# Attention on one core: the products with v of each half in two visits instead of one

## The chip, the cores and the metric

The kernel runs on one core of a Trainium2 chip. The metric is the device time of one execution in microseconds (us), the median of several runs. The program is one launch; the host only lays out the inputs.

## What is computed

The reference is an attention followed by two feed-forward parts. The change lies in the attention alone:

```python
scores = scale * np.matmul(q, k.transpose(0, 1, 3, 2))
thresh = np.max(scores, axis=-1, keepdims=True) - tau
scores = np.where(scores >= thresh, scores, -1000000000.0)
scores = scores - np.max(scores, axis=-1, keepdims=True)
attn = np.exp(scores)
attn = attn / (np.sum(attn, axis=-1, keepdims=True) + 1e-09)
return np.matmul(attn, v).astype(np.float32)
```

with 4 batches, 8 heads, 576 tokens and 64 columns per head, all float32. Its result goes as 2304 rows of 512 into a dense layer (512 to 2048 to 512, with a Mish between) and that into a soft mixture of eight small networks.

## The kernel before

The heads are worked in pairs: 16 pairs (NPR) of two heads, head 0 and head 1. A pair has 9 steps, one per chunk of 128 query rows: chunks 0 to 3 of either head, alternating, and a ninth chunk that holds the last 64 rows of both heads. The loop at L551 runs over 144 steps and 9 more that drain the pipeline; `j` is the step within a pair, `n` the pair.

The order of the work on every engine is the order in which the code issues it (`manual_schedule`), so the loop's body is the schedule. In step `i`:

- **Score group** (`emit_S`, L307), PE: negated scores of the chunk against all 576 keys, 4 matmuls of 288 columns (10 in the ninth chunk), into one of three two-bank tiles `s` (pool `ps_s`). The tile is used again three steps later, so a score group waits until the weighing of three steps before has read it.
- **Turn** (`emit_T`, L360), PE: four transposes of the weights of chunk `i - 3` (T_LAG), for keys 0 to 511, into a bank `tp` (pool `ps_t`, two banks); ACT copies it to `pT` (L94, a helper's line).
- **Reduce** (`emit_E`, L317) on DVE, the row's extreme `nm`, and after it the exp on ACT (L318).
- **Weighing** (`emit_P`, L340), DVE, of the chunk before: threshold times exp into `pab` (three buffers, each for two chunks) or, for the ninth chunk, `pr`. Then `th` (L324), a small step of DVE.
- **Tail turns** (`emit_R`, L375 and L377), PE: the last 64 keys of up to four chunks, turned together, three times a pair (part 0 in step 6, parts 1 and 2 in steps 2 and 3 of the next pair, R_AT). They go to the unused columns of the step's own `s` tile, ahead of its score group, and ACT copies them to `pTr` at the end of the step (`evac_R`).
- **Products with v** (`emit_V`, L399), PE: for half 0 (256 rows per head) and half 1 (320 rows) of a pair, five groups of keys by two heads, ten matmuls with 64 weight columns, summed in one `tp` bank, which ACT then copies to `xT`. The profile shows two records for each matmul. `pv_at` is called at three places in every step (z = 0 before the tail turns, z = 1 after the score group, z = 2 at the end); PV_0 and PV_1 name the place. Half 0 stands at the end of step 0 of the next pair, half 1 at the end of its step 4.

Around this, POOL prepares the next pair's k and q, DVE and ACT convert the first three blocks of the dense layer's weights in some steps (CONV, CVN: L161, L164, L169), and after the last pair of a batch the sums' reciprocals are turned on PE (`norm_b`, L419; NORM_AT), go through DRAM and come back as factors. After the 16 pairs the dense layer follows (L483 to L485, L647 to L649), in the drain its first matmuls stand between the last turns and products.

Of the kernel before, what the change touches and what calls it, by code (L numbers as in the profile page):

```python
# [8 lines left out]
F32 = mybir.dt.float32  # L9
# [15 lines left out]
NPR = B * NP  # L25
# [7 lines left out]


T_LAG = 3
PV_0 = 29
PV_1 = 14
R_AT = (6, 2, 3)
NORM_AT = (0, 4)
CONV = (4, 6, 13, 15, 22, 24, 31)  # L40
CVN = (9, 45, 81)
DRAIN = (1, 2, 7, 8, 3)
# [22 lines left out]
def pow2(n):  # L65

    return 1 << (n.bit_length() - 1)
# [3 lines left out]
def kernel(  # L71
# [21 lines left out]
    def copy_act(dst, src):  # L93
        act.activation(out=dst, in_=src, func=ACTF.Copy)  # L94
# [7 lines left out]
    tp = ctx.enter_context(tc.tile_pool(name="tp", bufs=2))  # L102
# [5 lines left out]
    ps_t = ph2.enter_context(tc.tile_pool(name="ps_t", bufs=2, space=PSUM))  # L108
# [75 lines left out]
    def spans(t0, n):  # L184
        a = t0
        while a < t0 + n:
            blk = a // BT
            e = min(t0 + n, (blk + 1) * BT)
            yield blk, a - blk * BT, a - t0, e - a
            a = e  # L190
# [194 lines left out]
            copy_act(tr[:64, 256:320], ps[:64, 0, :64])  # L385
            copy_act(tr[64:, 256:320], ps[64:, 1, 64:])

    def emit_V(n, half):

        b, hp = divmod(n, NP)  # L390
        w = 256 if half == 0 else 320
        t, tr = pT[n, half]
        vt, vrt = V[n]
        pv = ps_t.tile([128, 512], F32, name="tp")
        for kc in range(5):
            for h in range(2):
                hs = slice(64 * h, 64 * h + 64)
                lhsT, rhs = (vt[:, kc, h], t[:, kc, h]) if kc < 4 else (vrt[:, h], tr)
                pe.matmul(pv[hs, :w], lhsT=lhsT, rhs=rhs, start=(kc == 0), stop=(kc == 4))  # L399
        for blk, x0, p0, ln in spans(b * S + 256 * half, w):  # L400
            copy_act(xT[blk][:, hp, x0:x0 + ln], pv[:, p0:p0 + ln])

    def pv_at(i, z):

        n, k = divmod(3 * i + z, 27)
        for nn, half, place in ((n, 0, PV_0), (n - 1, 0, PV_0), (n - 1, 1, PV_1)):
            if place == k + 27 * (n - nn) - 27 * half and 0 <= nn < NPR:
                emit_V(nn, half)

    def norm_a(b):  # L410
        r = p1.tile([128, 36], F32, name="rr", bufs=2)
        dve.tensor_scalar(out=r, in0=rs[b], scalar1=1e-9, scalar2=None, op0=ALU.add)
        dve.reciprocal(out=r, in_=r)
        rinv[b] = r

    def norm_b(b, i):
        o = SH if i < NCH else 0
        ps = st[i]["s"][:36, 0, o:o + 128]
        pe.transpose(ps, rinv[b], ident)  # L419
        return lambda: norm_out(b, ps)  # L420
# [80 lines left out]
    with tc.manual_schedule():  # L501
# [49 lines left out]
        for i in range(NCH + 9):  # L551
            n, j = divmod(i, 9)
            live = i < NCH
            if live or j in R_AT[1:]:
                st[i] = {"s": ps_s.tile([128, 2, 512], F32, name="s")}
            R = None
            pv_at(i, 0)
            if n < NPR and j == R_AT[0]:
                R = (n, 0, i)
            if n >= 1 and j in R_AT[1:]:  # L560
                R = (n - 1, R_AT.index(j), i)
            if R:
                emit_R(*R)
            turn_out = None
            if n >= 1 and (n - 1) % NP == NP - 1:
                if j == (NORM_AT[1] if n < NPR else R_AT[2]):
                    turn_out = norm_b((n - 1) // NP, i)
            if live:
                emit_S(i)
            pv_at(i, 1)  # L570
            if T_LAG <= i < NCH + T_LAG:
                emit_T(i - T_LAG)
# [4 lines left out]
            if live:  # L577
# [11 lines left out]
                for m in range(NWA):  # L589
# [3 lines left out]
                    if z in CONV:  # L593
                        cv[m][CONV.index(z)]()
                        if z == CONV[-1] and m + 1 < NWA:
                            early_w(m + 1)
            pv_at(i, 2)
            if n >= 1:
                m = n - 1
                b, hp = divmod(m, NP)  # L600
                if hp == NP - 1 and j == (NORM_AT[0] if n < NPR else 0):
                    norm_a(b)
# [273 lines left out]
        for c0, w in COLS:  # L876
            n = pow2(1024 // w)
# [104 lines left out]
        for g in range(NF, NG, 2):  # L982
            blk, m = divmod(g, NF)
            prev = [g - 1] if g == NF else [g - 2, g - 1]
            plan = TRIPLES_0 if g == NF else TRIPLES_1 if m == 2 else TRIPLES
# [387 lines left out]
```

## Time and profile before

| | |
|---|---|
| median of 3 runs | 755.63 us (754.92 to 756.26) |
| the profiled execution | 755.94 us, its span 754.2 us |
| granted clock of TensorE, mean | 0.99 |
| PE busy | 728.1 us (97%) |
| DVE, ACT, POOL busy | 519.9, 459.1, 391.9 us |

PE is the matmul row, PEld its weight loads, which partly overlap the matmuls. A matmul's end is modelled, so the distance from start to start is the better measure of what PE takes. In rows of the timeline, the text in brackets is the idle time before the row and what ended it; a row with x4 stands for four instructions that follow each other. The first 300 us are the attention, the rest the two feed-forward parts.

### The profile page before, as it was taken

The numbers are of one execution on the slowest core, as the hardware profiler recorded it, in microseconds if no ns is written. First come the engines' busy times: TensorE is split into PE (matmuls) and PEld (weight loads), VectorE is DVE, ScalarE is ACT, GpSimd is POOL, SyncE is SP. The second block draws the span as 40 slices with busy tenths as digits, with TensorE's granted clock in tenths as the row PEclk, the third lists the DMA queues.
The fourth block names the chain that finished last, engine by engine and source line by source line (L and its number), as shares of the span: only waits on it lengthen the run. The fifth ranks groups of instructions, "written<-read, shape, count | busy, mean of one in ns | idle before, by whom it ended". The sixth has DMA issues, their size and how long they took to land.

```text
span 754.2 us, 12760 instructions
## 1 busy us (share of the span) xinstructions
PE 728.1 (97%) x4641; PEld 596.0 (79%) x4641; DVE 519.9 (69%) x1018; ACT 459.1 (61%) x880; POOL 391.9 (52%) x395
## 2 busy tenths in 40 slices
PE   8999999999999999999999999999999999999995
PEld 6777777777777778998999888887898888898443
DVE  7888888888888883656986756568867545754413
ACT  6877787777777775444464655566646555644213
POOL 6665567666647733333645755465755454544000
PEclk8999999999999999999999999999999999999998
DMA  7422443433313203343330100000006111259798
GB/s 246 134 81 83 154 127 98 124 126 107 128 56 97 81 4 126 113 143 137 112 112 1 63 1 1 1 1 0 1 1 232 69 57 56 94 218 370 251 397 296
DMA packets 45678, 84.85 MB, mean 113 GB/s; under 512 B 6048, under 2 KB 21040, under 8 KB 45616
## 3 DMA queue, kind: packets, MB, share of 16 engines
q1 hardware_dynamic: 45344, 83.88, 32.8%
q8 instruction: 36, 0.59, 0.3%
q14 instruction: 26, 0.21, 0.1%
q10 hardware_dynamic: 272, 0.16, 0.1%
HBM read 79.23 MB, written 4.79 MB: 111 GB/s over the span
## 4 chain that ended last, share of the span: by engine, by line
PE 75%; DVE 13%; issue 6%; ACT 5%; DMA 1%; SPq 0%; POOL 0%; ACTq 0%
PE tp L399 11%; PE s L647 8%; PE s L649 8%; PE s L648 8%; DVE pab L340 7%; PE s L307 7%; PE tp L742 5%; PE tp L744 4%; PE tp L743 4%; PE tp L483 3%; PE tp L485 3%; PE tp L484 3%; PE tp L360 2%; PE hp L1195 2%; DVE nm L317 2%
## 5 line engine op out<-in xcount | busy, mean ns | idle before, releaser
L307 PE MATMUL s<-kb,Q 128*128 128x288 f32 (+2 forms) x672 | 126.0, 316 | 10.2 <-DVE pab L340 4.6
L317 DVE TENSOR_REDUCE nm<-s 128x1 f32<-128x576 f32 x144 | 108.0, 750 | 38.8 <-PE s L307 38.6
L307 PEld LDWEIGHTS s<-kb,Q 128*128 128x128 f32 x672 | 95.1, 192 | 37.0 <-DVE pab L340 15.5
L466 POOL TENSOR_TENSOR wo<-wr,wo 128x512 fp32r<-128x512 f32 x48 | 68.5, 1426 | 99.2 <-ACT wo L94 85.5
L318 ACT ACTIVATE e<-s,nm 128x576 f32<-128x576 f32 x144 | 106.5, 740 | 18.7 <-DVE nm L317 15.2
L647 PE MATMUL s<-wo,gg 128*128 128x512 f32 x288 | 115.8, 402 | 0.8 <-DVE big L657 0.7
L649 PE MATMUL s<-wo,gg 128*128 128x512 f32 x288 | 114.0, 396 | 0.0
L648 PE MATMUL s<-wo,gg 128*128 128x512 f32 x288 | 113.8, 395 | 0.0
L340 DVE SCALAR_TENSOR_TENSOR pab<-s,th,e 128x576 f32<-128x576 f32 x128 | 103.5, 808 | 1.7 <-ACT pTr L94 1.7
L94 ACT ACTIVATE pT<-tp 128x512 f32<-128x512 f32 x144 | 86.2, 598 | 24.6 <-PE tp L360 24.1
L360 PE MATMUL tp<-ident,pab 128*128 128x128 f32 x512 | 78.6, 276 | 0.1
L399 PE MATMUL tp<-pT,vt 128*64 128x320 f32 (+1 forms) x512 | 69.1, 412 | 0.4 <-ACT pT L94 0.3
L732 POOL TENSOR_TENSOR wi<-wr,wi 128x256 fp32r<-128x256 f32 x48 | 47.3, 986 | 41.6 <-ACT wi L94 41.5
L753 ACT ACTIVATE hs<-hs 128x384 f32<-128x384 f32 x64 | 33.4, 522 | 56.5 <-DVE hs L1031 35.7
L732 POOL TENSOR_TENSOR wi<-ev,wi 128x256 fp32r<-128x256 f32 x64 | 52.5, 831 | 23.8 <-ACT wi L94 23.8
L649 PEld LDWEIGHTS s<-wo,gg 128*128 128x128 f32 x288 | 54.4, 189 | 12.6
L360 PEld LDWEIGHTS tp<-ident,pab 128*128 128x128 f32 x512 | 62.2, 142 | 0.8 <-issue 0.7
L647 PEld LDWEIGHTS s<-wo,gg 128*128 128x128 f32 x288 | 54.5, 189 | 9.8 <-issue 1.8
L648 PEld LDWEIGHTS s<-wo,gg 128*128 128x128 f32 x288 | 54.6, 190 | 7.5 <-POOL wo L466 0.4
L756 DVE TENSOR_TENSOR gg<-hs,gg 128x384 fp32r<-128x384 f32 x64 | 54.5, 852 | 7.6 <-ACT gg L94 7.6
L91 POOL TENSOR_SCALAR kb<-kr,kscale 128x576 fp32r<-128x576 f32 x30 | 22.5, 750 | 61.6 <-PE s L307 61.6
L399 PEld LDWEIGHTS tp<-pT,vt 128*64 128x64 f32 x512 | 33.9, 136 | 24.9 <-issue 5.1
(284 smaller groups left out, 1572.0 us busy)
## 6 DMA issues: line engine op xcount, KB each, us to landing
kr<-in_k SPq DMA_DIRECT2D x32, 288.0 KB, 3.0
qr<-in_q SPq DMA_DIRECT2D x32, 288.0 KB, 3.2
big<-in_w SPq DMA_DIRECT2D x15, 512.0 KB, 7.1
wr<-in_w SPq DMA_DIRECT2D x14, 512.0 KB, 3.3
big<-in_w_in SPq DMA_DIRECT2D x10, 512.0 KB, 4.8
big<-in_w_out SPq DMA_DIRECT2D x10, 512.0 KB, 5.0
wr<-in_w SPq DMA_DIRECT2D x13, 352.0 KB, 8.3
big<-in_w SPq DMA_DIRECT2D x13, 320.0 KB, 6.9
```

The lines of the kernel that those rows point to most:

```text
L94: act.activation(out=dst, in_=src, func=ACTF.Copy)
L307: pe.matmul(s[:, f, a:z], lhsT=t[:, o:o + 128], rhs=kb[:, hh, ko:ko + z - a], start=(j == 0), stop=(j == len(plan) - 1 and z == SH),)
L317: dve.tensor_reduce(out=nm, in_=s, axis=AX.XY, op=ALU.min)
L318: act.activation(out=e, in_=s, func=ACTF.Exp, bias=nm[:, 0:1], scale=-1.0)
L340: dve.scalar_tensor_tensor(out=p.rearrange("p (a b) -> p a b", a=2), in0=d["s"][:, :, :SH], scalar=d["th"][:, 0:1], in1=d["e"], op0=ALU.is ...
L360: pe.transpose(ps[:, kc], p[:, ko:ko + 128], ident)
L399: pe.matmul(pv[hs, :w], lhsT=lhsT, rhs=rhs, start=(kc == 0), stop=(kc == 4))
L466: pool.tensor_tensor(out=t[:, 1], in0=src, in1=t[:, 0].bitcast(F32), op=ALU.subtract)
L647: pe.matmul(ps, lhsT=hi[:, ts], rhs=w[:, 0], start=(m == 0), stop=False)
L648: pe.matmul(ps, lhsT=hi[:, ts], rhs=w[:, 1], start=False, stop=False)
L649: pe.matmul(ps, lhsT=lo[:, ts], rhs=w[:, 0], start=False, stop=(m == NF - 1))
L732: pool.tensor_tensor(out=lo, in0=src, in1=hi.bitcast(F32), op=ALU.subtract)
```

## The change

Each half's ten matmuls are issued in two visits. The first takes key groups 0 to 2 (six matmuls), the second groups 3 and 4 (four matmuls). The sum stays in its `tp` bank between them. Half 0 is visited at the start of step 1 of the next pair (place 30) and after the score group of step 2 (place 34); half 1 at the end of step 4 (place 41) and after the score group of step 6 (place 46). Tail turns: part 0 moves from step 6 to step 8, part 1 from step 2 to step 4 of the next pair, part 2 stays. The turn of the reciprocals moves from step 4 to step 5.

```diff
-PV_0 = 29
-PV_1 = 14
-R_AT = (6, 2, 3)
-NORM_AT = (0, 4)
+PV = ({30: (0, 1, 2), 34: (3, 4)}, {41: (0, 1, 2), 46: (3, 4)})
+R_AT = (8, 4, 3)
+NORM_AT = (0, 5)
...
-    def emit_V(n, half):
+    pvs = {}
+
+    def emit_V(n, half, kcs):
...
-        pv = ps_t.tile([128, 512], F32, name="tp")
-        for kc in range(5):
+        if kcs[0] == 0:
+            pvs[half] = ps_t.tile([128, 512], F32, name="tp")
+        pv = pvs[half]
+        for kc in kcs:
...
+        if kcs[-1] < 4:
+            return
...
-        for nn, half, place in ((n, 0, PV_0), (n - 1, 0, PV_0), (n - 1, 1, PV_1)):
-            if place == k + 27 * (n - nn) - 27 * half and 0 <= nn < NPR:
-                emit_V(nn, half)
+        for half, plan in enumerate(PV):
+            for back in range(2):
+                if k + 27 * back in plan and 0 <= n - back < NPR:
+                    emit_V(n - back, half, plan[k + 27 * back])
```

On PE, half 0 of the second pair, from the turn of step 0 to the turn of step 2 (vt and vrt are v, pT and pTr the turned weights). Before:

```order
L360 MATMUL tp<-ident,pab 128x128 x4
L399 MATMUL tp<-pT_442,vt 64x256 x8
L399 MATMUL tp<-pTr_443,vrt 64x256 x2
L307 MATMUL s<-kb,Q_0_109 128x288 x2
L307 MATMUL s<-kb,Q_0_111 128x288 x2
L360 MATMUL tp<-ident,pab 128x128 x4
L375 MATMUL s<-ident,pab 128x128 x2
L307 MATMUL s<-kb,Q_0_109 128x288 x2
L307 MATMUL s<-kb,Q_0_111 128x288 x2
L360 MATMUL tp<-ident,pr 128x128 x4
```

And after the change, the same stretch:

```order
L359 MATMUL tp<-ident,pab 128x128 x4
L403 MATMUL tp<-pT_439,vt 64x256 x6
L306 MATMUL s<-kb,Q_0_109 128x288 x2
L306 MATMUL s<-kb,Q_0_111 128x288 x2
L359 MATMUL tp<-ident,pab 128x128 x4
L306 MATMUL s<-kb,Q_0_109 128x288 x2
L306 MATMUL s<-kb,Q_0_111 128x288 x2
L403 MATMUL tp<-pT_439,vt 64x256 x2
L403 MATMUL tp<-pTr_440,vrt 64x256 x2
L359 MATMUL tp<-ident,pr 128x128 x4
```

Four of the ten matmuls now stand behind the second score group, ahead of a turn, and the tail turn of this stretch has gone.

On DVE, steps 3 and 4 of the second pair, with the engines whose semaphores each instruction waits for (PE, Activation is ACT). Before:

```order
L317 TENSOR_REDUCE nm<-s 128x1 [waits PE_49]
L340 SCALAR_TENSOR_TENSOR pab,rs<-s,th,e 128x576 [waits DVE_49,Activation_49]
L324 TENSOR_SCALAR th<-nm,tau_eff 128x1 [waits DVE_49]
L317 TENSOR_REDUCE nm<-s 128x1 [waits PE_49]
L340 SCALAR_TENSOR_TENSOR pab,rs<-s,th,e 128x576 [waits DVE_49,Activation_49]
```

And after the change:

```order
L316 TENSOR_REDUCE nm<-s 128x1 [waits PE_49]
L339 SCALAR_TENSOR_TENSOR pab,rs<-s,th,e 128x576 [waits DVE_49,PE_49,Activation_49]
L323 TENSOR_SCALAR th<-nm,tau_eff 128x1 [waits DVE_49]
L316 TENSOR_REDUCE nm<-s 128x1 [waits PE_49]
L339 SCALAR_TENSOR_TENSOR pab,rs<-s,th,e 128x576 [waits DVE_49,Activation_49]
```

The order is the same, but the weighing of step 3 now waits for PE too: it writes the buffer that the tail turn of step 4 reads. The weighing of step 7 has the same new wait, for the tail turn of step 8.

## Rows read from the trace of the kernel before

**Rows 1.** Windows: busy us (instructions) of PE, PEld, DVE, ACT, POOL; clock; DMA
```profile
21.70:264.20 242.50, 234.50 (x1741) 180.81 (x1739) 206.26 (x529) 186.61 (x355) 158.81 (x158) 1.00 0.34 108
300.00:620.00 320.00, 315.86 (x1636) 280.21 (x1636) 216.00 (x281) 175.59 (x342) 166.83 (x148) 0.99 0.18 61
```

**Rows 2.** The page's costliest groups, and the waits of PEld (us, times, longest)
```profile
L317 DVE TENSOR_REDUCE nm<-s 128x1 f32<-128x576 f32 x144 | 108.0, 750 | 38.8 <-PE s L307 38.6
...
PEld s L307 <- DVE pab L340: 15.0, 42, 0.5
```

**Rows 3.** Timeline, steps without products: start, length, engine, line
```profile
100.83 0.56 PEld L307 LDWEIGHTS s<-kb,Q 128*128 128x128 f32 x4 [0.49 <-issue]
...
101.67 0.76 DVE L317 TENSOR_REDUCE nm<-s 128x1 f32<-128x576 f32 x1 [1.73 <-PE s L307]
...
102.34 0.81 DVE L340 SCALAR_TENSOR_TENSOR pab<-s,th,e 128x576 f32<-128x576 f32 x1
...
103.20 0.75 DVE L317 TENSOR_REDUCE nm<-s 128x1 f32<-128x576 f32 x1
103.21 0.56 PEld L307 LDWEIGHTS s<-kb,Q 128*128 128x128 f32 x4 [0.19 <-DVE pab L340]
```

**Rows 4.** Timeline, the products of half 0
```profile
107.16 0.49 PEld L360 LDWEIGHTS tp<-ident,pab 128*128 128x128 f32 x4
...
107.81 1.49 PEld L399 LDWEIGHTS tp<-pT,vt 128*64 128x64 f32 x16 [0.17 <-issue]
...
109.59 0.60 PE L399 MATMUL tp<-pTr,vrt 128*64 128x256 f32 x4
110.12 0.56 PEld L307 LDWEIGHTS s<-kb,Q 128*128 128x128 f32 x4 [0.38 <-POOL kb L91]
...
110.96 0.76 DVE L317 TENSOR_REDUCE nm<-s 128x1 f32<-128x576 f32 x1 [1.24 <-PE s L307]
```

**Rows 5.** Timeline, the products of half 1, and the reduce after those of another pair
```profile
115.18 1.81 PEld L399 LDWEIGHTS tp<-pT,vt 128*64 128x64 f32 x16 [0.17 <-issue]
...
117.39 0.71 PE L399 MATMUL tp<-pTr,vrt 128*64 128x320 f32 x4
118.03 0.56 PEld L307 LDWEIGHTS s<-kb,Q 128*128 128x128 f32 x4 [0.49 <-DVE big L164]
...
170.78 0.76 DVE L317 TENSOR_REDUCE nm<-s 128x1 f32<-128x576 f32 x1 [1.67 <-PE s L307]
```

**Rows 6.** Timeline, the ninth chunk's score group, and weight loads back to back
```profile
104.73 1.32 PEld L307 LDWEIGHTS s<-kb,Q 128*128 128x128 f32 x10 [0.53 <-DVE pab L340]
...
106.00 0.42 PEld L360 LDWEIGHTS tp<-ident,pab 128*128 128x128 f32 x4
...
118.53 0.49 PEld L360 LDWEIGHTS tp<-ident,pab 128*128 128x128 f32 x4
118.99 0.25 PEld L375 LDWEIGHTS s<-ident,pab 128*128 128x128 f32 x2
119.21 0.57 PEld L307 LDWEIGHTS s<-kb,Q 128*128 128x128 f32 x4
```

**Rows 7.** Timeline of DVE, the reduce of step 0 in four pairs
```profile
21.70 0.75 DVE L317 TENSOR_REDUCE nm<-s 128x1 f32<-128x576 f32 x1
...
73.92 0.75 DVE L317 TENSOR_REDUCE nm<-s 128x1 f32<-128x576 f32 x1
...
90.83 0.75 DVE L317 TENSOR_REDUCE nm<-s 128x1 f32<-128x576 f32 x1
...
264.22 0.75 DVE L317 TENSOR_REDUCE nm<-s 128x1 f32<-128x576 f32 x1
```

**Rows 8.** Timeline of PEld, products in the drain, behind the reciprocals' turn
```profile
289.43 1.81 PEld L399 LDWEIGHTS tp<-pT,vt 128*64 128x64 f32 x16 [0.21 <-issue]
```

**Rows 9.** Timeline, a turn and its copy
```profile
101.34 0.49 PEld L360 LDWEIGHTS tp<-ident,pab 128*128 128x128 f32 x4
...
102.10 0.60 ACT L94 ACTIVATE pT<-tp 128x512 f32<-128x512 f32 x1 [0.71 <-PE tp L360]
```

## The prediction, made before the changed kernel ran

> **What bounds the kernel now.** I began with the windows of the whole program. The stretch with all its pairs of heads in full swing (21.7 to 264.2 us) is a third of the time, and there PE shows 234.5 of 242.5 us busy, at a granted clock of 1.00 (2.4 GHz) [rows 1]. From 300 us on PE is busy 315.9 of 320 us, and the change touches nothing there. So the question is whether PE is really full in the first stretch. A busy PE is not PE at its peak, so I read the waits next: DVE's reduce waits 38.6 us for score groups of PE, and PE's weight loads wait 15.0 us, 42 times, for DVE's weighing (L340) [rows 2]. Both engines wait for each other, so neither is full, and the order of the work costs time.
>
> The timeline shows how. Without products, DVE sets the pace: from reduce to reduce 1.53 us (101.67 to 103.20) [rows 3]. PE needs less: a score group 0.50 us and a turn 0.46 us back to back, 0.96 in all [rows 5, 6], so it could gain 0.57 us per step. It may not, because a score group needs the bank of three steps before. From the start of a weighing to the score group that it frees are 0.87 us (102.34 to 103.21), from score group to reduce 0.84 (100.83 to 101.67), together 1.71; DVE itself comes to that reduce 0.86 + 1.53 = 2.39 us after the weighing's start [rows 3]. PE can therefore be 0.68 us ahead and no more.
>
> Now the products. Half 0 holds PE for 2.31 us (107.81 to 110.12), and the turn ahead of it takes 0.65 instead of 0.46, with 0.17 idle: entering costs 0.19 [rows 4]. PE falls back 2.50, gets back 0.57 of the step and 0.68 of lead: DVE should stand still for 1.25 us. It reads 1.24 [rows 4]. Half 1 holds 2.85 us (115.18 to 118.03): 2.85 + 0.19 - 1.25 = 1.79, and it reads 1.67 [rows 5]. So the holes are the long blocks, and between the blocks PE waits at its lead's limit.
>
> **The change, part by part.** A pair takes 17.32 us (21.70 to 264.22, 14 pairs) [rows 7]. PE's own work in one:
> - 8 score groups of 0.505: 4.04; the last one, of ten matmuls, 104.73 to 106.00: 1.27 [rows 6]
> - 9 turns of 0.46: 4.14; 3 tail turns of 0.22 (118.99 to 119.21): 0.66
> - products 2.31 + 2.85 = 5.16, entering 2 x 0.19 = 0.38
>
> Sum 15.65, so PE waits 1.67 us per pair. DVE's own steps are 9 x 1.53 = 13.77, plus the weight conversion's passes: a pair without them takes 16.91 (73.92 to 90.83) [rows 7], so about 0.4 of the 17.32 is theirs.
>
> *Two visits.* Half 0 comes as 12 and 8 of its 20 records, half 1 the same. A record of half 0 is 0.111 us (16 from 107.81 to 109.59), 20 are 2.22, and the block is 2.31: leaving costs 0.09 [rows 4]. For half 1 it is 0.1375, 2.75 and 2.85: 0.10 [rows 5]. The change adds two visits per pair, each with a leaving and an entering. Leaving: 0.09 to 0.10. Entering now follows a score group, which the trace never shows; bounds are 0 (a turn follows a score group at no loss, 118.53) and 0.21 (the entering after the reciprocals' turn, 289.43) [rows 6, 8]. I take the 0.17 of the two usual entries, since both kinds of neighbour that the trace has pay about that. That is 2 x (0.09 + 0.17) = 0.52, between 0.18 and 0.62. The Trainium skill (TensorEngine Tiling (Array Packing), Key Properties) has a rule that speaks against the change here: a change of the tiling mode, and not of the tile alone, drains TensorE; the products are 64 columns wide, their neighbours 128. By that rule every visit pays on both sides, and the sum would stay at my 0.52 or go to 0.62; by the row of the unhindered turn alone it would fall to 0.18. The trace's 0.17 to 0.21 at entries agrees with the rule so far.
>
> *Does PE still wait?* Walk through the steps, with 0.57 won per step. The first visit of half 0 (1.33 + 0.09 + 0.19 = 1.61) makes PE late. The second (0.89 + 0.26 = 1.15) and the tail turns of steps 3 and 4 (0.22 each) leave it a lead of at most 0.35 before half 1's first visit (1.94). Step 5 gives 0.57, the second visit in step 6 (1.37) takes it. Step 7 gives 0.57, the tail turn now in step 8 (0.22) and the long score group (0.77 more) take it. The lead stays under 0.68, so PE no longer waits for DVE: the pair becomes PE's own work, 15.65 + 0.52 = **16.17 us**, 1.15 less. DVE's holes then sum to about 16.17 - 13.77 = 2.4 us, in four or five places of 0.2 to 1.0, and the conversion passes fall into them. If they don't, up to 0.2 per pair comes back.
>
> *Tail turns moved.* The weighing of step 3 writes a pab buffer that the tail turn of step 4 still reads, so DVE now waits for PE there, and in step 7 for the tail turn of step 8; behind it in DVE's queue stand th and the next reduce. Price: after a score group starts, DVE reaches that weighing at 0.84 + 0.67 = 1.51. PE ends the group at 0.50, the turn at 0.96, and the tail turn is readable about 0.57 later, estimated as the second transpose's 0.11 plus the 0.46 from a last score matmul to its reduce (0.84 less three spacings of 0.127): 1.53. So 0.02 us, with 0.35 behind it before anything on PE is late. I take 0; bounds 0 and 0.3 each.
>
> *One bank for turns.* While a half's sum stays in its bank, the turns have one bank: each waits for the copy of the one before. Turn start to copy is 0.76 and the copy 0.60 [rows 9], so the next turn may start 1.4 us later. Between the two turns lie a score group and a visit, 0.50 + 0.89 + 0.26 = 1.65 at least: covered, if ACT isn't late. If it is, the rival below. A half's copy now comes in steps 2 and 6 ahead of a turn's copy and an exp on ACT; ACT is busy 186.6 of 242.5 us [rows 1], I take 0. Nothing on SP and POOL is passed; POOL has 158.8 of 242.5.
>
> *Sum.* Fifteen pairs hold products: 15 x 1.15 = 17.25. In the first pair the tail turn enters step 8: -0.22. The last pair's visits stand in the drain, among matmuls that keep PE full: -0.52. Gain 16.5. The profiled execution took 755.94: 739.4. It lies 0.31 over the median of the runs shown, so **739.1 us**.
>
> **Rivals.**
> - *Free visits* (entering and leaving cost nothing more): 15 x 1.67 - 0.22 = 24.8, so 730.8. For it: turn and score group follow each other at no loss. Against: every entry in the trace pays.
> - *The new waits bite*: 0.25 each, two per pair, over 16 pairs: +8, so 747. For it: the margin is 0.02 and rests on an estimate. Against: 0.35 of lead behind it.
> - *ACT sets the turns* (slower): with one bank, a turn that finds ACT in an exp (0.74) ahead of the copy (0.60) waits 1.34; the tail turn behind it, and with it the weighing, are late, in two places per pair (steps 3 and 7). Less 0.35 of lead: 2 x 0.99 x 16 = 32, so 771. It decides from 0.52 us per place on (16.5 / 16 / 2). For it: each turn in a visit's stretch now names ACT's last copy. Against: ACT has 56 us free in the stretch and two score groups of time. [...]
> - *Given back*: the rest of the program waits for something with a time of its own, 755. Against: its weights are requested and converted relative to the end of the pairs, and PE is 99% busy there [rows 1].
>
> **How the numbers follow.** Forecast 0.56, free visits 0.17, waits 0.16, ACT 0.06, given back 0.05. The range takes in the first three with their bounds: 730.5 to 748. What a measurement can tell from no change is about 0.2%, 1.5 us: faster 0.89, same 0.05, slower 0.06.
>
> **What would show it.** Right: pairs of 16.0 to 16.3 us; PE's waits for the weighing nearly gone; DVE's waits for score groups down from 38.6 to some 25 us, in more and smaller pieces; entries of second visits with 0.1 to 0.2 idle. Wrong: weighings that wait for L374 or L376, turns that wait for ACT's copies, or a pair over 17 us.

## The result, and the profile after

| | before | after |
|---|---|---|
| median | 755.79 us (754.92 to 756.26, 4 runs) | 741.96 us (741.68 to 743.48, 4 runs) |
| profiled execution, its span | 755.94, 754.2 us | 741.77, 740.0 us |

The ratio is 0.982, with a 95% interval of 0.981 to 0.984: 13.8 us faster. The forecast was 739.1 us, with a range of 730.5 to 748, so it was right, and 2.9 us too low.

The windows of the changed kernel, from the reduce of step 0 in pair 1 to that in pair 15 (the columns are those of [rows 1]):

```profile
21.82:251.71 229.89, 228.81 (x1743) 176.70 (x1743) 213.97 (x529) 182.62 (x354) 158.44 (x157) 1.00 0.36 114
```

The same 14 pairs took 242.50 us before [rows 1]. By the profile's busy time PE now idles for 1.08 us of them in all; before it was 8.0. The group of the reduce on the page, and four of the waits:

```profile
L316 DVE TENSOR_REDUCE nm<-s 128x1 f32<-128x576 f32 x144 | 108.1, 751 | 18.3 <-PE s L306 16.9
L339 DVE SCALAR_TENSOR_TENSOR pab<-s,th,e 128x576 f32<-128x576 f32 x128 | 103.4, 808 | 0.2 <-ACT pTr L93 0.2
```

```profile
PEld tp L359 <- ACT e L317: 10.3, 24, 0.5
PEld tp L403 <- issue: 9.7, 58, 0.2
...
PEld s L306 <- DVE th L323: 5.4, 11, 0.5
...
PEld s L306 <- DVE pab L339: 1.4, 3, 0.5
```

Over the whole program, DVE's wait for score groups fell from 38.6 to 16.9 us, and the loads of score groups, which had waited 15.5 us for the weighing (15.0 of them in [rows 2]), wait 1.4. The weighings themselves, which got a new wait for the tail turns, stood idle for 0.2 us in the whole program. The two longest lines need care. The timeline of PEld over one pair shows what they are:

```profile
102.16 0.49 PEld L359 LDWEIGHTS tp<-ident,pab 128*128 128x128 f32 x4
102.81 1.06 PEld L403 LDWEIGHTS tp<-pT,vt 128*64 128x64 f32 x12 [0.17 <-issue]
104.26 0.57 PEld L306 LDWEIGHTS s<-kb,Q 128*128 128x128 f32 x4 [0.39 <-issue]
104.77 0.49 PEld L359 LDWEIGHTS tp<-ident,pab 128*128 128x128 f32 x4
105.23 0.57 PEld L306 LDWEIGHTS s<-kb,Q 128*128 128x128 f32 x4
105.97 0.20 PEld L403 LDWEIGHTS tp<-pT,vt 128*64 128x64 f32 x4 [0.17 <-issue]
106.24 0.36 PEld L403 LDWEIGHTS tp<-pTr,vrt 128*64 128x64 f32 x4
106.98 0.42 PEld L359 LDWEIGHTS tp<-ident,pr 128*128 128x128 f32 x4 [0.39 <-ACT e L317]
107.37 0.25 PEld L376 LDWEIGHTS s<-ident,pr 128*128 128x128 f32 x2
...
109.96 1.27 PEld L403 LDWEIGHTS tp<-pT,vt 128*64 128x64 f32 x12 [0.17 <-issue]
111.72 0.56 PEld L306 LDWEIGHTS s<-kb,Q 128*128 128x128 f32 x4 [0.49 <-DVE th L323]
```

Behind every visit the loader idles 0.39 (half 0) or 0.49 us (half 1), whether the row names "issue", an exp of ACT or th of DVE. PE is at the last products then. What the row names had ended only a little before (the exp at 106.76, 0.22 us ahead of the turn; th at 111.57, 0.15 ahead of the score group), but the instruction does not use it: the turn needs the bank whose copy was done at 106.14, and the score group a bank that an earlier weighing had read. The idle time is also the same where the row names "issue", and before the change ([rows 4, 5], 0.38 and 0.49). So these lines of the waits are the ends of visits, not a new bottleneck. The 0.17 ahead of each visit is the entering; the line "PEld tp L403 <- issue" counts 58 of them, against 30 before.

What the visits cost can be read in the same rows. Entering from a score group: 105.23 to 105.97 is 0.74, less the 0.51 that a score group takes when a turn follows, 0.23. From a turn: 102.16 to 102.81, 0.65 less 0.46, 0.19. Leaving: 102.81 to 104.26 is 1.45, less 12 records of 0.111, 0.12. The turn behind a second visit gives a little back (106.98 to 107.37, 0.39 instead of 0.46).

The time went where the forecast put it, but not evenly. The intervals between the reduces of step 0 are the pairs:

```profile
21.82 0.75 DVE L316 TENSOR_REDUCE nm<-s 128x1 f32<-128x576 f32 x1
...
38.05 0.75 DVE L316 TENSOR_REDUCE nm<-s 128x1 f32<-128x576 f32 x1
...
54.33 0.75 DVE L316 TENSOR_REDUCE nm<-s 128x1 f32<-128x576 f32 x1
...
234.85 0.75 DVE L316 TENSOR_REDUCE nm<-s 128x1 f32<-128x576 f32 x1
...
251.71 0.75 DVE L316 TENSOR_REDUCE nm<-s 128x1 f32<-128x576 f32 x1
```

The 14 pairs from 21.82 to 251.71 take 16.42 us on average, 0.90 less than before [rows 7]. Ten of them take 16.1 to 16.3 (the first two shown: 16.23, 16.28), and four are longer by about 0.6: pairs 6, 10, 13 and 14, counted from 0 (16.83, 16.97, 16.85, 16.86). Two separate causes stand in the timeline. In pairs 6 and 10 a pass of DVE that converts weights runs beside POOL, here in step 4 of pair 6:

```profile
111.24 1.42 POOL L237 TENSOR_TENSOR Q<-qr,Q 128x576 fp32r<-128x576 f32 x1
...
111.49 1.72 DVE L163 SCALAR_TENSOR_TENSOR big<-big 128x512 uint32<-128x512 uint32 x1
112.64 1.18 POOL L90 TENSOR_SCALAR ks<-kr,kscale 128x576 f32<-128x576 f32 x1
113.13 0.74 DVE L316 TENSOR_REDUCE nm<-s 128x1 f32<-128x576 f32 x1
```

The pass takes 1.72 instead of 0.68 us, and the next reduce stands behind it; both pairs have another pass in step 6. PE shows it at the end of the pair: from the turn behind the ninth chunk's score group to the next score group it takes 0.76 us (117.61 to 118.37), in clean pairs 0.39. (A pass slowed in the same way, at 144.38 in pair 8, cost that pair only 0.1: it has no second one.) In the last pairs POOL itself is late with q:

```profile
232.91 1.83 POOL L463 TENSOR_TENSOR big<-big 128x768 fp32r<-128x768 f32 x1 [3.05 <-ACT big L93]
...
235.47 1.42 POOL L237 TENSOR_TENSOR Q<-qr,Q 128x576 fp32r<-128x576 f32 x1
236.01 0.30 PEld L306 LDWEIGHTS s<-kb,Q 128*128 128x128 f32 x2 [0.39 <-issue]
...
236.94 0.30 PEld L306 LDWEIGHTS s<-kb,Q 128*128 128x128 f32 x2 [0.64 <-POOL Q L237]
```

The score group of step 1 is issued in two halves, the second waits 0.64 us for q's low part, and that stands in POOL's queue behind the low part of the dense layer's input (L463), which waited 3.05 us for ACT.

### The profile page after: what moved, and what is told of

The parts are those of the page before. It is cut to its first block, busy times and chain, and to the rows that moved or that the text cites. A ratio compares the mean times of both kernels' runs of the same rounds, so it can differ in the third digit from the quotient of the medians.

```text
span 740.0 us, 12760 instructions
## 1 busy us (share of the span) xinstructions
PE 720.1 (97%) x4641; PEld 589.3 (80%) x4641; DVE 528.0 (71%) x1018; ACT 454.7 (61%) x880; POOL 391.8 (53%) x395
## 4 chain that ended last, share of the span: by engine, by line
PE 85%; DVE 5%; ACT 4%; issue 2%; POOL 2%; DMA 1%; SPq 0%; ACTq 0%
PE tp L403 10%; PE s L306 10%; PE s L654 8%; PE s L656 8%; PE s L655 8%; PE tp L359 8%; PE tp L749 5%; PE tp L751 5%; PE tp L750 5%; PE tp L490 3%; PE tp L492 3%; PE tp L491 3%; PE hp L1202 2%; PE so L1234 2%; DVE pab L339 1%
## 5 line engine op out<-in xcount | busy, mean ns | idle before, releaser
L316 DVE TENSOR_REDUCE nm<-s 128x1 f32<-128x576 f32 x144 | 108.1, 751 | 18.3 <-PE s L306 16.9
L403 PE MATMUL tp<-pT,vt 128*64 128x320 f32 (+1 forms) x512 | 76.0, 418 | 0.4 <-ACT pT L93 0.4
L656 PEld LDWEIGHTS s<-wo,gg 128*128 128x128 f32 x288 | 54.1, 188 | 12.5
L93 ACT ACTIVATE wi<-wr 128x256 fp32r<-128x256 f32 (+1 forms) x63 | 29.3, 465 | 37.7 <-DVE wr L168 22.6
L403 PEld LDWEIGHTS tp<-pT,vt 128*64 128x64 f32 x512 | 31.1, 136 | 23.9 <-issue 9.7
```

What stands on the lines that cost most here:

```text
L316: dve.tensor_reduce(out=nm, in_=s, axis=AX.XY, op=ALU.min)
L656: pe.matmul(ps, lhsT=lo[:, ts], rhs=w[:, 0], start=False, stop=(m == NF - 1))
```

## Experiments

The theory: PE's own work sets the pair now, about 16.2 us with four visits, and before it was the long blocks of products, each of which let DVE run dry. Rivals: the moved tail turns made the gain; the longest block still sets the pace; PE has room left. In each group of runs the kernel before ran on the same chip; the ratios are to it. "Pair" is the mean of the 14 pairs from pair 1 to pair 15, in the profiled execution.

| kernel | us | ratio (95%) | pair |
|---|---|---|---|
| before | 755.79 | 1 | 17.32 |
| changed | 741.96 | 0.982 (0.981 to 0.984) | 16.42 |
| old tail turns, both halves split | 744.72 | 0.987 (0.985 to 0.989) | 16.60 |
| only half 1 split | 746.08 | 0.989 (0.986 to 0.991) | 16.67 |
| only half 0 split | 753.94 | 0.999 (0.998 to 1.001) | 17.27 |
| only half 0 split, old tail turns | 750.87 | 0.994 (0.993 to 0.996) | 17.09 |
| three visits per half | 752.17 | 0.997 (0.996 to 0.998) | 17.06 |
| two visits, the short one first | 743.09 | 0.985 (0.983 to 0.987) | 16.46 |
| changed, more work on PE | 746.58 | 0.990 (0.989 to 0.991) | 16.72 |
| before, more work on PE | 755.55 | 1.002 (1.001 to 1.003) | 17.32 |
| changed, dense input in step 7 | 739.20 | 0.980 (0.979 to 0.982) | 16.33 |
| the same and passes moved | 739.67; again 739.09 | 0.980 (0.979 to 0.982); 0.980 (0.978 to 0.982) | 16.26; 16.25 |
| changed, beside that second run | 741.10 | 0.982 (0.980 to 0.984) | 16.41 |

### More work on PE, in the changed kernel and in the one before

```diff
+            if live and j in (3, 7):
+                spare_ps = st[i]["s"][:, :, SH:SH + 128]
+                for y in range(2):
+                    pe.transpose(spare_ps[:, y], ident, ident)
```

The changed kernel:

> The changed kernel with four transposes more per pair on PE (two in step 3, two in step 7, of the identity into columns that nobody reads; nothing is left out): 0.44 us of PE per pair, 7.0 us in 16 pairs. Theory (after the change PE's own work sets the pair): the whole of it shows, pairs of 16.67 us, 748 to 749 us in all. Rival (DVE's holes set the pair, PE still has room): 742 to 743 us.

The kernel before:

> The kernel before with the same four transposes more per pair. Theory (there PE waits 1.67 us per pair at its lead's limit, in steps 1 to 3 and 5 to 8): they fall into PE's waits, and the time stays within 2 us of 755.8. Rival (PE was the bound before already, and the split helped in another way): 762 to 763 us.

Windows of the same 14 pairs, the changed kernel with the added transposes:

```profile
22.20:256.24 234.04, 233.71 (x1797) 182.64 (x1797) 212.44 (x529) 183.56 (x354) 157.42 (x157) 1.00 0.36 112
```

And the kernel before with them:

```profile
22.91:265.42 242.51, 238.56 (x1799) 186.44 (x1797) 206.20 (x529) 186.41 (x355) 158.41 (x158) 1.00 0.34 108
```

In the kernel before, the 14 pairs take 242.51 instead of 242.50 us: PE's busy time rose by 4.06 and the pairs not at all. The ratio in the table, 1.002, lies a little above 1; in the profiled execution 1.2 us stand ahead of the first pair (its first reduce comes at 8.77 instead of 7.59), where the other runs scatter from 7.6 to 8.7 us. The waits show where the work went. Over the whole program the loads had waited for the weighing for 15.5 us ahead of score groups and 2.9 ahead of the tail turn of step 3, 18.4 together. Now 6.0 stand ahead of the added transposes and 5.6 ahead of the score groups, 6.8 us less, and the added work is 16 x 0.44 = 7.0:

```profile
PEld s L565 <- DVE pab L340: 6.0, 31, 0.2
PEld s L307 <- DVE pab L340: 5.6, 16, 0.4
```

In the changed kernel the 14 pairs grow by 4.15 us (0.30 a pair). Pairs that were clean show most of the 0.44, 16.5 to 16.7 instead of 16.1 to 16.3. The last two, where PE had waited for POOL, show 0.2, and pairs 6 and 10, where PE waits behind the slowed pass of DVE, nothing (16.81 and 16.93). So the whole came to 4.6 us by the medians and 5.7 by the ratios, and not to the 6 to 7 expected. The theory holds for the clean pairs, and this is the plainest sign of it: the same work is free before and paid after.

### More visits, and other sizes of visit

```diff
-PV = ({30: (0, 1, 2), 34: (3, 4)}, {41: (0, 1, 2), 46: (3, 4)})
+PV = ({30: (0, 1), 32: (2,), 34: (3, 4)}, {41: (0, 1), 44: (2,), 46: (3, 4)})
```

> Both halves in three visits of 2, 1 and 2 key groups instead of two. Theory (PE is full in a pair, a visit more costs what it takes to enter and leave, about 0.3 us): two visits more per pair, 0.6 us, pairs of 16.85 us in place of 16.23, 750 to 752 us in all. Rival (the longest block still sets the time by DVE's holes): shorter blocks, smaller holes, 736 to 742 us. Rival (a visit costs nothing and PE has room): 742 us.

Two reduces of step 0, and the wait line that counts entries:

```profile
55.75 0.75 DVE L316 TENSOR_REDUCE nm<-s 128x1 f32<-128x576 f32 x1
...
72.64 0.75 DVE L316 TENSOR_REDUCE nm<-s 128x1 f32<-128x576 f32 x1
```

```profile
PEld tp L403 <- issue: 14.8, 89, 0.2
```

A clean pair is 16.89 us, 0.66 more than with two visits, so 0.33 for each visit added, entering and leaving together. Most of the gain of the change is gone, though every block is shorter. The last two pairs, at 18.0, also waited longer for POOL's q: 1.06 us instead of 0.64. The entries went from 58 to 89. A visit of the same number but another size:

```diff
-PV = ({30: (0, 1, 2), 34: (3, 4)}, {41: (0, 1, 2), 46: (3, 4)})
+PV = ({30: (0, 1), 34: (2, 3, 4)}, {41: (0, 1), 46: (2, 3, 4)})
```

> The changed kernel with two key groups in the first visit and three in the second, for both halves. Theory (the number of visits, not the length of the longest one, sets the pair once PE is full): clean pairs stay at 16.2 to 16.3 us, 742 us in all. Rival (the layout is a fine balance, and the second visit ahead of a turn is the tight place): clean pairs of 16.5 us or more, 746 us or more.

The clean pairs are 16.19 to 16.25 us, so the size of the two visits does not matter to PE's sum. The last two pairs are 17.29 (16.85 in the changed kernel): with a shorter first visit step 1's score group asks for q earlier, and POOL brings it no sooner (a wait of 1.04 us instead of 0.64). These two are 0.9 us of the 2.0 by which the whole is longer than the changed kernel's run beside it (741.10). The rest isn't in the 14 pairs: in the profiled executions the first of them begins 1.2 us later (22.47 against 21.25).

### One half alone

Half 1 alone:

```diff
-PV = ({30: (0, 1, 2), 34: (3, 4)}, {41: (0, 1, 2), 46: (3, 4)})
+PV = ({29: (0, 1, 2, 3, 4)}, {41: (0, 1, 2), 46: (3, 4)})
```

> Only half 1's products are split; half 0's ten matmuls stand in one block at the end of step 0, tail turns as in the changed kernel. Theory (a long block lets DVE run dry, and between blocks PE can't work ahead by more than 0.68 us): half 0's block of 2.5 us leaves a hole as in the kernel before, so half the gain goes: pairs of about 16.8 us, 748 to 751 us in all, and PE's waits for the weighing come back in the steps ahead of the block. Rival (only the longer block of half 1 mattered): pairs of 16.2 to 16.3 us, within 2 us of the changed kernel's 742.

Half 0's block, in the timeline of DVE from the reduce of step 0 to the next:

```profile
88.58 0.75 DVE L316 TENSOR_REDUCE nm<-s 128x1 f32<-128x576 f32 x1
91.54 0.76 DVE L316 TENSOR_REDUCE nm<-s 128x1 f32<-128x576 f32 x1 [1.35 <-PE s L306]
```

The hole is there, as before the change (1.24, [rows 4]), and so are PE's waits for the weighing, now mostly ahead of the tail turns (6.4 and 5.8 us). But the pair is 16.6, not 16.8: splitting half 1 alone brings 0.65 of the 0.90. I had split the gain evenly, and the halves are not alike.

Half 0 alone, with the changed tail turns (half 1 then has to start in step 5, behind their copy), and in the kernel before with nothing else changed:

```diff
-PV = ({30: (0, 1, 2), 34: (3, 4)}, {41: (0, 1, 2), 46: (3, 4)})
+PV = ({30: (0, 1, 2), 34: (3, 4)}, {42: (0, 1, 2, 3, 4)})
```

> Only half 0's products are split; half 1's ten matmuls stand in one block at the start of step 5, tail turns as in the changed kernel. Theory (a long block lets DVE run dry and PE can't work ahead of it by more than 0.68 us; half 1's is the longer of the two): DVE's hole of some 1.7 us stays, clean pairs of 16.9 to 17.1 us, 751 to 754 us in all. Rival (splitting either half gives the same, since either leaves one long block): clean pairs of 16.6 us as with half 1 alone split, 746 to 748 us.

```diff
-PV = ({30: (0, 1, 2), 34: (3, 4)}, {41: (0, 1, 2), 46: (3, 4)})
-R_AT = (8, 4, 3)
-NORM_AT = (0, 5)
+PV = ({30: (0, 1, 2), 34: (3, 4)}, {41: (0, 1, 2, 3, 4)})
+R_AT = (6, 2, 3)
+NORM_AT = (0, 4)
```

> The kernel before with half 0's products alone in two visits; half 1 in one block, tail turns and reciprocals at their old steps, so that the products of half 1 have no copy to wait for (in the run with half 0 split and the tail turns moved they waited 0.24 us per pair for it). Theory (half 1's block is the longer one and keeps its hole in DVE of about 1.7 us; the split of half 0 takes away a hole of 1.24 and costs one visit of 0.3): pairs of 16.8 to 17.0 us, 748 to 751 us in all, half 1's hole in every pair at 1.5 to 2.0 us. Rival (splitting either half is worth the same, so only the wait for the copy held that run back): pairs of 16.6 us, 745 to 747 us.

With the changed tail turns, timeline over half 1's block in pair 3:

```profile
81.31 1.81 PEld L403 LDWEIGHTS tp<-pT,vt 128*64 128x64 f32 x16 [0.17 <-issue]
81.32 0.74 DVE L316 TENSOR_REDUCE nm<-s 128x1 f32<-128x576 f32 x1
...
83.36 0.30 PEld L403 LDWEIGHTS tp<-pTr,vrt 128*64 128x64 f32 x4 [0.24 <-ACT pTr L93]
...
85.01 0.76 DVE L316 TENSOR_REDUCE nm<-s 128x1 f32<-128x576 f32 x1 [1.48 <-PE s L306]
```

From reduce to reduce 3.69 us: a hole of 2.16 beyond the 1.53 of a step (in the kernel before 3.34, from 98.33 to the reduce at 101.67 of [rows 3], a hole of 1.81). The products waited 0.24 for the copy of the tail turns. That is so in most pairs, but in pairs 1, 5 and 9 the wait is 1.26 or 1.27 and the pair takes 18.0 us (7.0 us of waits in all, not 0.24 per pair), and this run gained nothing. Without that wait the split of half 0 saves 0.23 us a pair, less than the 0.3 to 0.5 expected. One block is left, and the weighing waits are still there (11.6 us, 32 times, of 15.5). So both splits with the moved tail turns bring 0.90, half 1's split with the moved turns 0.65, half 0's with the old ones 0.23. No run has the moved turns and neither half split, so how much of the 0.65 is theirs is not shown; with both halves split the move is worth 0.18 (below). If it were as much here, half 1's long block would still be the dearer one, as its hole said.

### The tail turns

```diff
-R_AT = (8, 4, 3)
-NORM_AT = (0, 5)
+R_AT = (6, 2, 3)
+NORM_AT = (0, 4)
```

> The changed kernel with its products in two visits, but the tail turns and the turn of the reciprocals at their old steps (6, 2, 3 and 4). Theory (PE's own work sets the pair, and the order only has to keep PE supplied): PE's work is the same, so pairs without a fault of their own stay near 16.2 us and the time is 742 to 747 us; what the moved tail turns saved is the wait of weighings in the last pairs, where ACT is late with its copies. Rival (the gain came from moving the tail turns, and not from splitting the products): the time goes back to 750 us or more.

Pairs of 16.4 to 16.5 and three of 17.1 to 17.2 at the end. In those the weighing itself waits:

```profile
234.72 0.82 DVE L339 SCALAR_TENSOR_TENSOR pab<-s,th,e 128x576 f32<-128x576 f32 x1 [0.97 <-ACT pTr L93]
```

A tail turn in step 6 has its copy on ACT behind the dense layer's input, which ACT also copies in step 6. Of the 0.90 per pair, 0.72 stay without any tail turn moved, so the split makes most of the gain and the moves add 0.18. The clean pairs are 0.15 to 0.2 longer too, which I had not expected. The trace shows one place for it, at the end of the pair:

```profile
101.51 0.82 DVE L339 SCALAR_TENSOR_TENSOR pab<-s,th,e 128x576 f32<-128x576 f32 x1 [0.24 <-ACT pTr L93]
101.91 0.42 PEld L359 LDWEIGHTS tp<-ident,pab 128*128 128x128 f32 x4
...
102.45 0.56 PEld L306 LDWEIGHTS s<-kb,Q 128*128 128x128 f32 x4
```

The weighing is late by 0.24, and the score group that needs its bank starts 0.94 us after it, at the end of PE's lead. From this turn to this score group PE takes 0.54 to 0.57 in the clean pairs, and 0.38 to 0.45 in those of the changed kernel, where the tail turn (0.22) stands in step 8, just ahead. So the moved tail turn falls into time in which PE would stand.

### The last pairs, and the two passes

```diff
-                if 11 <= m < 15 and j == 6:
+                if 11 <= m < 15 and j == 7:
```

> The changed kernel with the high and low part of the dense layer's input (ACT and POOL, in pairs 11 to 14) issued in step 7 instead of 6, so that POOL has the last part of the next q in its queue ahead of them. Theory (in the last pairs the second half of step 1's score group waits 0.6 us for POOL's q, which stands behind an operation that waits for ACT): pairs 12 to 15 fall from 16.85 to 16.3 us, 739.8 to 740.5 us in all. Rival (the last pairs are long for ACT's or DVE's own load there): pairs 12 to 15 stay at 16.8, 742 us.

POOL and PE at the place where the second half of the score group had waited:

```profile
233.56 1.82 POOL L463 TENSOR_TENSOR big<-big 128x768 fp32r<-128x768 f32 x1 [2.52 <-ACT big L93]
...
235.37 0.74 POOL L90 TENSOR_SCALAR ks<-kr,kscale 128x576 f32<-128x576 f32 x1
235.55 0.57 PEld L306 LDWEIGHTS s<-kb,Q 128*128 128x128 f32 x4 [0.39 <-POOL big L463]
```

The operation still waits for ACT, but q's low part is already done ahead of it, and the four loads of the score group follow each other. Pairs 13 and 14 fall from 16.85 to 16.23 and 16.24. (Pair 12, which the expectation counted among the long ones, was 16.3 before already.)

```diff
-CONV = (4, 6, 13, 15, 22, 24, 31)
+CONV = (4, 9, 13, 18, 22, 27, 31)
...
-                if 11 <= m < 15 and j == 6:
+                if 11 <= m < 15 and j == 7:
```

> The same move of the dense layer's input to step 7, and the weight conversion's passes of step 6 in step 0. Theory (pairs 6 and 10 are 0.6 us long because a pass of DVE in step 6 runs beside POOL's work and takes 1.7 instead of 0.7 us, while PE stands behind the second visit): pairs 6 and 10 fall to 16.3 as well, 738.5 to 739.5 us in all, faster than the changed kernel by 2.5 to 3.5 us. Rival (the passes are slow wherever they stand): 740 to 742 us.

Here the expectation named the wrong pass. The slowed ones stand in step 4, and the edit leaves them there; what it takes out of the pair is the second pass, in step 6. Pair 6 kept its slowed pass and fell from 16.83 to 16.54:

```profile
112.34 1.41 POOL L237 TENSOR_TENSOR Q<-qr,Q 128x576 fp32r<-128x576 f32 x1
...
112.41 1.90 DVE L163 SCALAR_TENSOR_TENSOR big<-big 128x512 uint32<-128x512 uint32 x1
```

Pair 10 fell to 16.23, because there, by less than 0.1 us, the pass came first:

```profile
177.61 0.68 DVE L163 SCALAR_TENSOR_TENSOR big<-big 128x512 uint32<-128x512 uint32 x1
177.69 1.88 POOL L237 TENSOR_TENSOR Q<-qr,Q 128x576 fp32r<-128x576 f32 x1
```

Now the pass takes 0.68 and POOL's operation 1.88 instead of 1.42. So the rival (the passes are slow wherever they stand) is wrong, and so is the theory's reason in part: who starts first decides who is slow. The 14 pairs take 16.26 us on average, and the time is that of the kernel that only moves the input, within what the runs scatter. Because the two stood so close, this kernel and the changed one ran once more side by side:

> The kernel with the dense layer's input in step 7 and the passes of step 6 in step 0, once more, beside the changed kernel. Theory (its pairs are shorter by 2.3 us in all, 16.26 instead of 16.42): 1.5 to 3 us less than the changed kernel. Rival (its gain comes back behind the pairs): the same time as the changed kernel within 1 us.

> The changed kernel itself once more, beside the kernels of this group: 741 to 743 us, clean pairs of 16.23 us, pairs 6 and 10 and the last three at 16.8 to 17.0.

739.09 us (738.44 to 740.66) against 741.10 (740.16 to 741.59): 2.0 us less, as the pairs say (14 x (16.41 - 16.25) = 2.2). The ranges overlap a little, so this is faster than the changed kernel by little more than the measurement can tell, and faster than the kernel before by 15.2 us. It is the fastest version here, together with the one that only moves the input.

## Why the prediction was right, and where it was off

- **What bounds before** (a third of the time in a stretch where PE and DVE wait for each other, holes at the long blocks): right. The added work on PE was free there and the hole of an unsplit block stays where it was. The two waits read for it reach further than the stretch: in the stretch itself they are 35.1 us (38.6 in the whole program) and 13.9 (15.0 up to 283 us).
- **PE's own work per pair, 15.65**, and **two more visits, 0.52**: right, somewhat low. The clean pairs are 16.23 against 16.17. By the rows a visit enters for 0.19 to 0.23, not 0.17 (the sum counted 0.19 for the old entries and only their idle 0.17 for the new ones), and leaves for 0.12, not 0.09 to 0.10; three visits put the price of one at 0.33 where the sum had 0.26. Entering from a score group, which the trace of before did not show, is the dearer of the two. The rule of the Trainium skill (TensorEngine Tiling (Array Packing), Key Properties) that a change of tiling mode drains TensorE agrees with this: every visit added paid on both sides, and the row of the unhindered turn (no cost) did not hold. *Free visits* falls with it.
- **Does PE still wait?** No for the weighing: 15.5 us fell to 1.4. The holes of DVE are 16.9 us by the reduce's row and not some 25; the direction was right. DVE has less idle time than I counted partly because its passes grew: eight of them, slowed to between 0.8 and 1.9 us, make it busy for 6.0 us more than at 0.42 and 0.68 each.
- **Tail turns moved, 0**: right. The weighings waited 0.2 us in the program, so *the new waits bite* falls. The move is even worth 0.18 us a pair by the run with the old places, which the sum did not count by itself.
- **One bank for turns, 0**: right. The loads of products or turns that name ACT's copy of pT sum to less than 2 us, and *ACT sets the turns* falls.
- **The sum** was where it was off: 15 pairs x 1.15, and the traces give 0.90. In the 14 pairs from pair 1 that is 3.5 us: 0.8 are the dearer visits (14 x 0.06), 1.3 the two pairs with a pass slowed beside POOL (16.83 and 16.97), 1.3 the last two that waited for q. The sentence that failed is "Nothing on SP and POOL is passed; POOL has 158.8 of 242.5". POOL has time in the whole stretch, but in the last pairs its queue holds an operation that waits for ACT, and a PE that comes 0.6 us sooner to step 1 finds q not ready. The forecast did leave room for a part of this ("if they don't, up to 0.2 per pair comes back", of the passes); the passes cost 0.1 a pair on average.
- **First pair**: the sum had 0.22 of loss. The reduce of step 0 in pair 1 comes 0.12 later than before in one run of the changed kernel (21.82 against 21.70) and 0.45 earlier in the other (21.25), so no run resolves it.
- **Last pair and drain**: the total fell by 14.2 us in the profiled executions, 12.5 of it up to the reduce of step 0 in pair 15. Pair 15, the last that holds products, fell from 16.21 to 15.24 us between its first and its last reduce, which is 0.97 of the forecast's 1.15. Behind its last reduce the span takes 473.8 us before and 473.1 after, 0.7 less, where the sum had 0.52 more. That is luck: the rest takes 473.8 to 474.0 us in the three profiled executions whose mean granted clock from 400 to 500 us was 0.98 (before, before with more work on PE, and the first run of the kernel with passes moved), and 471.7 to 473.1 in the others, where it was 1.00. So in these two executions 1.2 us of the forecast's nearness are not owed to its reasons, and the 0.52 for the drain is neither borne out nor refuted.
- *Given back*: no. The 12.5 us gained up to pair 15 are still there at the end.

One more reading was wrong, though the sum did not use it: the pair of 16.91 us (73.92 to 90.83, [rows 7]) is not without passes.

```profile
82.90 0.68 DVE L169 SCALAR_TENSOR_TENSOR wr<-big 128x512 uint32<-128x512 uint32 x1
```

That pass stands in step 4, ahead of the hole of half 1. The pairs with a pass in step 6 take 17.27 us or more, and pairs 13 and 14, which have no pass but carry the dense layer's input, 17.33. So the 0.4 put down to the passes, and the 0.2 that might come back, were worked out from no pair without them.

## What to carry to other kernels

When two engines wait for each other, count the own work of each over one period and compare the sum with the period: the gap is what an order can bring, and the splits that close it are paid per cut (here about 0.3 us each), so the smallest number of cuts that removes the holes is the best. Adding work that nobody reads to the suspected engine tells at once whether it has room: free before, paid after. And an engine that is far from busy in the whole stretch can still be the next bound at the one place where its queue holds something that waits for another engine; look at the queue, not at the busy share.

## What had not been expected of the hardware

DVE's passes over two tensors in SBUF and POOL's operations lock each other out. Beside the low part of q on POOL (L237, 1.42 us), passes that started 0.07 to 0.25 us after it (L163, L168; 0.68 alone) took 1.72 (111.49), 1.76 (144.38) and 1.86 (177.01) in the changed kernel and 1.90 (112.41) in the last one. All four ended 0.55 or 0.56 us after POOL's operation, so they did not run at half speed: they stood until it was through. Where the pass started 0.08 us ahead (177.61 in the last kernel), it took its 0.68, and POOL's operation ended 1.28 us after it. The weighing, which reads scores from PSUM, averages 0.81 us over its 128 instances. The Trainium skill (SBUF — State Buffer, Who interferes with whom) states that a DVE instruction with two SBUF inputs contends with a GpSimd instruction that reads SBUF, and that "Issue order, not op shape, decides who blocks." The traces agree on both. A pass with one tensor (L160) was also held, 1.26 instead of 0.42 us (193.84); by the same section of the Trainium skill that takes a two-port mode of DVE, and no run here shows which mode it ran in. Before the change the passes met POOL's operation only near its end (0.88 and 0.98 us at worst), so a new order of the work on PE moved the meeting on two engines whose own order had not changed.
